# Stores of the last channels asked for on two queues, a broadcast read from 16 rows, and four pairs of loads joined

## The chip, the cores and the metric

The kernel runs on one core of one Trainium2 chip. The metric is the device time of one execution in microseconds. A profiled execution also has a span, from its first to its last instruction, which is a little shorter than its time. The engines are named as in the profile: PE is TensorE (PEld its weight loads), DVE is VectorE, ACT is ScalarE, POOL is GpSimd, SP is the sync engine. An engine name with a q (SPq, ACTq) stands for what the engine's own sequencer does, above all asking for transfers.

## What is computed

Two branches work on the same input of 2048 rows and 512 channels and are mixed by a gate:

```python
x = A_u
g = sigmoid((x * gate_w).sum(-1, keepdims=True))
a = state_space(x)        # kernel K[d, l] = Re sum_n C B dt exp(dt A l); y = irfft(rfft(K, 2L) * rfft(u, 2L))[:L] + u * Dskip
b = linear_attention(x)   # 32 heads of 16; phi = [softmax(p), softmax(-p)]; o = phi_q (phi_k^T v) / (phi_q . sum phi_k + 1e-6); o @ wo
return g * a + (1 - g) * b
```

In a, the convolution kernel has 2048 taps for each channel and comes from 128 complex states. In b, every query row is divided by its own normaliser, one number for each head.

## The kernel before, in words

**An order written out by hand.** The class `Plan` collects nodes: an engine, a function that issues instructions, what it depends on. `Plan.ORDER` is a string that holds the sequence of all nodes, two characters for each. Every engine executes its own nodes in this sequence, and a node that waits holds up what is behind it on its engine. Where a node may run on one of two engines, the next digit of `Plan.SIDES` picks the first (0) or the second (1). Digits are used up in the order in which the nodes were added, not in the order of execution. `Plan.dma` (line 128) adds a transfer as three nodes: the request, which an engine's sequencer issues, and two empty ones for its movement and its landing. In the kernel before, all transfers are requests on SP.

**The input's spectrum** is worked out early and written to the DRAM tensor XUd. Later `load` (line 1178) reads it back in tiles XUX of 128 x 2 x 1024. For the first three quarters of the channels, a tile comes in two requests of 256 KB at line 1186, and for the last quarter in two at line 1188: one request for each of the two halves `i`, which are the same rows shifted by 64.

**The attention queries** (`plan_queries`) run in four blocks of 512 rows. `block` takes exponentials (Eq), forms the sums of all heads in one PSUM tile, and works out on ScalarE and VectorE one factor for each row, head and sign: the normaliser apm, 128 partitions of 256 numbers. A partition stands for (i, h, m): the 128-row group i, head h of eight in a group, and m of four groups. It must be copied to all 16 features of a head. For this apm is written to DRAM (apd, line 895) and read back (ax, line 902): one load for each i, in which each of 8 rows of 1024 numbers is read 16 times. VectorE then multiplies Eq by ax (line 909), two multiplications for each block. Block 3 is the late one, and its stores are at line 991.

**The convolution** (`plan_conv`) runs over the channels in chunks of 32 (units 0 to 15). `kgen` builds the taps (matmuls at line 179) and their spectrum, `transform` multiplies by XUX (line 1289, 1292 or 1227), goes back through psz (line 1315) and stores the result in DRAM (Zd, line 1330), from where ZT is read (line 1349) with other axes on the partitions. The matmuls at line 1378 finish the inverse transform on top of what the attention left, VectorE multiplies by the gate (line 1389) into xT, and the stores at line 1400 write xT to the output. Quarters 0 to 2 hold four units each. The last quarter is split: units 12 and 13 together, then 14, then 15. There are two groups of stores in it, four requests each: after units 12 and 13 for their 64 channels, and after unit 15 for the 64 channels of 14 and 15. One request takes 32 of the 128 partitions and writes 512 pieces of 128 bytes. Line 1400 uses ScalarE's queue when the node's engine is ACT and SP's otherwise; before the change no digit is spent on it and the engine is SP.

**The order around the end.** The last nodes are, in sequence: the stores of the earlier quarters, VectorE's transposes and multiplications by the gate, ScalarE's two last copies of Zr, the four stores of block 3 (line 991), the four of units 12 and 13, VectorE's last three multiplications (line 1389), and the last four stores.

Of the kernel before, what the change touches and what calls it, by code (L numbers as in the profile page):

```python
# [10 lines left out]
ACT = mybir.ActivationFunctionType  # L11
ALU = mybir.AluOpType
F32 = mybir.dt.float32
BF16 = mybir.dt.bfloat16
# [56 lines left out]
class Plan:  # L71
# [738 lines left out]
def plan_queries(P, nc, g, psum, r):  # L810

    fc, act, at, xT = g.fc, g.act, g.at, g.xT
# [12 lines left out]
    def block(b, late, yn=()):  # L825
# [68 lines left out]
        def aw():  # L894
            nc.sync.dma_start(out=g.apd[b].rearrange("i h m c -> (i h m) c"), in_=Q.apm[:].rearrange("p s t -> p (s t)"))
            Q.apm = None

        def ar(ip):
            if ip == 0:
                Q.ax = g.fpool.tile([128, 4, 4, 2, 128], BF16, name="ax", tag="ax", bufs=g.P.k["ax"])  # L900
            for i in (2 * ip, 2 * ip + 1):
                nc.sync.dma_start(out=Q.ax[:, i].rearrange("p m s t -> p (m s t)"),
                                  in_=g.apd[b, i].rearrange("h m c -> h (m c)").unsqueeze(1).to_broadcast([8, 16, 1024]))
        n = P.dma("aw" + L, 0.45, 2.0, aw, [n], drop=["nrm"], move=0.3)
        em, ld = [], None
# [9 lines left out]
        for ip in range(2):  # L915
            for mp in range(1 if late else 2):
# [21 lines left out]
                ot.append(evict("oT" + L, oe, [po, wo]))  # L938

        def out_mm(ps, i, j):  # L940
            for m in range(4):
                nc.tensor.matmul(ps, lhsT=g.oT[3][i // 2][:, m, 128 * (i % 2):128 * (i % 2) + 128], rhs=g.wo[:, m, :], start=(m == 0), stop=False,
                                 skip_group_check=True)
            nc.tensor.matmul(ps[:, 384:512], lhsT=xT[:, j, 3, :], rhs=at.diagD[:, 3, :], start=False, stop=True, skip_group_check=True)
            nc.tensor.matmul(ps[:, 0:384], lhsT=g.ident[:], rhs=g.Y[:, i].rearrange("p q d -> p (q d)"), start=False, stop=True, skip_group_check=True)
        if not late:
            box = Bag()

            def pbm(box=box):
                box.ps = g.heat(g.psA.tile([128, 4, 128], F32, name="bps", tag="bk"), 3)  # L950
                for i in range(4):
                    attn(box.ps[:, i], 4 * b + i, 3, i == 0, True)

            def bs(box=box):
                i = box.ps[:]
                box.ps = None
                return xT[:, 4 * b:4 * b + 4, 3, :], i
            pb = P.add("PE", "bpsq", pbm, ot + [wo], take=["bk"], rw=("diagD", ""))
            out.append(evict("bs3", bs, [pb] + g.xTr))
            g.ot[b] = ot + [wo]  # L960
        on = []
        for ip in range(2 if late else 0):
# [11 lines left out]
            def bg(k, j=j, box=box):  # L974
                o, i = xT[:, j + k, 0:3, :].rearrange("p k d -> p (k d)"), box.ps[:, k, 0:384]
# [12 lines left out]
        if late:  # L988
            def st(h):
                for c in (2 * h, 2 * h + 1):  # L990
                    (nc.scalar if P.cur.at == "ACT" else nc.sync).dma_start(out=g.out2d[:, 0:384].rearrange("(q j c) d -> c q j d", q=32, j=16, c=4)[c][:, 4 * b:4 * b + 4],
                                      in_=xT[32 * c:32 * c + 32, 4 * b:4 * b + 4, 0:3, :].rearrange("p j a d -> p j (a d)"))
# [38 lines left out]
def plan_exp(P, nc, g, psum, U, T, psq, deps):  # L1031
# [5 lines left out]
    def pe():  # L1037
        T.E = g.epool.tile([128, 2, 32, 32], BF16, name="E", bufs=g.P.k["E"])
        box.ps = psum([128, 2, 16, 32], "args")
        for e in range(2):  # L1040
            nc.tensor.matmul(box.ps[:, e], lhsT=g.statE[64 * e:64 * e + 64, h, :], rhs=g.selE[64 * e:64 * e + 64, 16 * cc:16 * cc + 16, :],  # L1041
                             start=True, stop=True, tile_position=(64 * e, 0))

    def ex():
        act(out=T.E[:, 1], in_=box.ps[:].rearrange("p e x t -> p (e x) t"), func=ACT.Exp)
        box.ps = None

    def el():
        nc.vector.tensor_tensor(out=T.E[:, 0].rearrange("p c (t k) -> p c t k", k=2), in0=T.E[:, 1].rearrange("p c (t k) -> p c t k", k=2),
                                in1=g.G[:, 32 * U:32 * U + 32].unsqueeze(2).to_broadcast([128, 32, 16, 2]), op=ALU.mult)  # L1050
# [5 lines left out]
def plan_conv(P, nc, g, psum, r):  # L1056
# [121 lines left out]
    def load(Q, p):  # L1178
        L = Bag()
        L.ring, L.left = "XUX", 2  # L1180

        def dma():
            L.X = g.fpool.tile([128, 2, 1024], BF16, name="XUX", tag="XUX", bufs=g.P.k["XUX"])
            for i in range(2):
                if Q < 3:
                    nc.sync.dma_start(out=L.X[:, i].rearrange("p (h z) -> p h z", h=2), in_=g.XUd[Q, :, 64 * i:64 * i + 128, 8 * p:8 * p + 8, :].rearrange("h x r c -> x h (r c)"))
                else:
                    nc.sync.dma_start(out=L.X[:, i], in_=g.XUd[Q, p // 2, 64 * i:64 * i + 128, 16 * (p % 2):16 * (p % 2) + 16, :].rearrange("x r c -> x (r c)"))
        src = [(h, 8 * p + 4) for h in range(2)] if Q < 3 else [(p // 2, 16 * (p % 2) + r) for r in (4, 12)]
        L.n = P.dma("xup", 0.9, 2.0, dma, [g.XUn[k] for k in src] + [sk], take=["XUX"], move=1.9, cnt=2)  # L1190
        return L

    def transform(XA, ready, Q, off, nd, Ls, last, co=0, free=True, split=False):
# [4 lines left out]
        nh, w = max(1, nd // 64), min(nd, 64)  # L1198
        pair = 1 if Q == 1 else 0
        lo = 64 if last else off  # L1200
# [151 lines left out]
        for j0 in range(0, 16, nj):  # L1352
# [3 lines left out]
            def pya(j0=j0, box=box):  # L1356
                box.ps = psum([128, 2, 512], "psy")
                box.py = box.ps[:].rearrange("p b (r d) -> p b r d", d=nd)
                for i in range(nj):
                    j, o = j0 + i, box.py[:, i // 4, i % 4]  # L1360
                    if j < 12:
# [22 lines left out]
            def ou(j0=j0, box=box):  # L1384
                gb = g.gT[:, j0:j0 + nj]
                if Q < 3 and j0:
                    nc.vector.tensor_tensor(out=bS[:, 8:12, do], in0=box.py[:, 0], in1=g.gT[:, 8:12].unsqueeze(2).to_broadcast([128, 4, nd]), op=ALU.mult)
                    return
# [8 lines left out]

            def st(h, js=slice(0, 12 if Q < 3 else 16)):
                for c in (2 * h, 2 * h + 1):
                    (nc.scalar if P.cur.at == "ACT" else nc.sync).dma_start(out=ov[c][:, js], in_=xT[32 * c:32 * c + 32, js, Q - pair:Q + 1, lo:off + nd].rearrange("p j a d -> p j (a d)"))  # L1400
            ya = []
            if Q < 3:
                ya = [P.add("PE", "pya", pya, [sq] + [n for b in range(j0 // 4, min(3, j0 // 4 + 2)) for n in g.ot[b]] + ([y] if j0 else []), take=[psq], rw=("diagD", ""))]
# [3 lines left out]
            two = Q < 3 and j0 > 0  # L1407
# [4 lines left out]
            if end and Q != 0 and (nd > 32 or last):  # L1412
                for h in range(2):
                    P.dma("out", 1.2, 2.0, lambda h=h, st=st: st(h), on, move=(1.6 if pair else 1.05 if nd == 128 else 0.9), cnt=2)
                on.clear()

    for h in range(6):
# [6 lines left out]
        done = done + kgen((2 * h, 2 * h + 1), XA, h % 2 == 0)  # L1424
        if h % 2:
            transform(XA, done, h // 2, 0, 128, [load(h // 2, p) for p in range(4)], False)
    for n in yn:
        n.deps.append(g.half)
    for u in range(12, 16):
        if u in g.PHASES:  # L1430
            phase(range(u, g.PHASES[u]))
    late += r["block"](3, True, yn)
    L, first = [load(3, p) for p in range(4)], None
# [11 lines left out]
def full_kernel(tc, A_u, A_A_re, A_A_im, A_B_re, A_B_im, A_C_re, A_C_im, A_log_dt, A_Dskip,  # L1445
                B_x, B_wqkv, B_w_phi, B_wo, gate_w, out):
    nc = tc.nc
# [5 lines left out]
    with ExitStack() as ctx:  # L1453
# [192 lines left out]
```

## Time and profile before

| | |
|---|---|
| median of 3 runs | 253.25 us (253.02 to 254.99) |
| time of the profiled execution | 253.31 us |
| its span | 251.4 us |
| TensorE clock granted | 0.961 of full speed |
| bytes moved by the DMA engines | 35.39 MB, mean 141 GB/s |

A timeline line reads: start in us from the start of the span, duration, engine, line of the kernel, operation, output<-input, count, and in brackets the idle time ahead of it and what ended that. For a transfer on SPq the duration is that of the request on the sequencer and not of the movement. A line of a list by tile gives the least, the median and the greatest duration in ns, and the first and the last start. A line of the stretches gives from and to, length, busy time of each engine with its count of instructions, then TensorE's granted clock, the mean busy share of the 16 DMA engines (transfers overlap, so it can pass 1) and GB/s. A line of a list of waits reads: who waited, for whom, us in total, times, the longest.

### The profile page before, as it was taken

How to read it: one execution, taken by the hardware profiler on the slowest of the kernel's cores; microseconds unless marked ns; L12 is line 12 of the kernel's file. 1: busy time of each engine (PE TensorE's matmuls, PEld its weight loads, DVE VectorE, ACT ScalarE, POOL GpSimd, SP SyncE). 2: the span in 40 equal slices, each digit the busy share in tenths (PEclk: the TensorE clock that was granted, in tenths of full speed). 3: DMA queues.
4: the chain of work that ended last, by engine and by line, in shares of the span. 5: the costliest groups of instructions: out<-in, count | busy, mean ns of one | idle time of the engine just before them, and what ended most of it. 6: DMA issues, size and time to landing. Idle time of an engine off the chain costs nothing.

```text
span 251.4 us, 9921 instructions
## 1 busy us (share of the span) xinstructions
PE 203.1 (81%) x4436; PEld 141.4 (56%) x4436; DVE 233.7 (93%) x322; ACT 222.4 (88%) x306; POOL 6.3 (3%) x15
## 2 busy tenths in 40 slices
PE   0567899999966378798878778899998789999970
PEld 0466655456743344255556646775667566777550
DVE  6799999999899997999999999999999999999690
ACT  6699899999989999999999999999999899975330
POOL 5310000000000000000000000000000000000000
PEclk9999999999997759999999999999999999999995
DMA  6799200037290488400325226904786678998775
GB/s 158 158 204 176 83 4 3 21 109 190 55 257 3 125 240 227 169 3 4 117 76 190 85 80 195 289 25 122 175 199 167 201 235 218 215 252 170 179 170 81
DMA packets 62122, 35.39 MB, mean 141 GB/s; under 512 B 41984, under 2 KB 57984, under 8 KB 61696
## 3 DMA queue, kind: packets, MB, share of 16 engines
q1 hardware_dynamic: 62080, 34.76, 54.5%
q8 instruction: 34, 0.56, 0.9%
q14 instruction: 8, 0.07, 0.1%
HBM read 21.91 MB, written 12.85 MB: 138 GB/s over the span
## 4 chain that ended last, share of the span: by engine, by line
ACT 34%; PE 23%; DVE 17%; DMA 10%; SPq 8%; issue 6%; ACTq 0%; DVEq 0%
ACT cs L68 8%; DMA ZT<-Zd 5%; ACT Eq L68 4%; ACT XA L145 4%; ACT E L68 4%; SPq L1512 4%; PE kps L179 3%; PE vp L753 3%; ACT L65 3%; PE pk L705 3%; PE psB L612 2%; DVE Zk L732 2%; ACT Zr L145 2%; SPq L212 2%; DMA UD<-in_A_u_dram 2%
## 5 line engine op out<-in xcount | busy, mean ns | idle before, releaser
L179 PEld LDWEIGHTS <-A 128*32 128x32 bf16 x1664 | 28.5, 160 | 6.6 <-issue 3.8
L179 PE MATMUL kps<-R,A 128*32 128x64 bf16 x1664 | 30.2, 228 | 2.2 <-issue 0.6
L68 ACT ACTIVATE cs<-args 128x1024 bf16<-128x1024 f32 x32 | 30.7, 1045 | 0.4 <-PE args L1019 0.3
L1118 DVE TENSOR_TENSOR R<-E,cs 128x2048 bf16<-128x2048 bf16 x16 | 19.5, 1216 | 0.0
L1097 DVE TENSOR_TENSOR A<-Ctab,Dtab 128x2048 bf16<-128x2048 bf16 x16 | 19.5, 1216 | 0.0
L1102 DVE TENSOR_TENSOR A<-Ctab,Dtab 128x2048 bf16<-128x2048 bf16 x16 | 19.5, 1216 | 0.0
L1114 DVE TENSOR_TENSOR R<-E,cs 128x2048 bf16<-128x2048 bf16 x16 | 19.5, 1216 | 0.0
L145 ACT CAST Zr<-psz 128x1024 bf16<-128x1024 f32 (+1 forms) x17 | 16.5, 974 | 2.5 <-issue 1.2
L145 ACT CAST XA<-psA 128x1024 bf16<-128x1024 f32 (+1 forms) x16 | 15.6, 1006 | 3.2 <-PE psA L186 3.2
L753 PE MATMUL vp<-WW,xT 128*128 128x512 bf16 x64 | 18.3, 416 | 0.0
L145 ACT CAST XK<-psB 128x1024 bf16<-128x1024 f32 (+1 forms) x15 | 15.1, 1010 | 3.4 <-PE psB L192 1.9
L612 PE MATMUL psB<-XAu,TB 64*128 64x128 bf16 x256 | 11.8, 249 | 7.3 <-ACT xst L145 5.1
L1289 DVE TENSOR_TENSOR t<-XUX,XK 128x2048 bf16<-128x2048 bf16 x14 | 17.0, 1217 | 0.6 <-ACT XK L145 0.6
L68 ACT ACTIVATE Ek<-pk 128x512 bf16<-128x512 f32 x32 | 16.8, 602 | 0.4 <-PE pk L705 0.2
L68 ACT ACTIVATE E<-args 128x1024 bf16<-128x1024 f32 x16 | 16.8, 1057 | 0.2 <-PE args L1041 0.2
L68 ACT ACTIVATE Eq<-pq 128x512 bf16<-128x512 f32 (+1 forms) x28 | 16.7, 710 | 0.2 <-PE pq L839 0.2
L1315 PE MATMUL psz<-t,TI 128*128 128x512 bf16 x60 | 15.2, 379 | 1.4 <-ACT cs L68 0.5
L839 PE MATMUL pq<-xT,Wqp 128*128 128x512 bf16 x64 | 15.6, 380 | 0.6 <-ACT Eq L68 0.6
L705 PE MATMUL pk<-WW,xT 128*128 128x512 bf16 x64 | 16.0, 380 | 0.0
L612 PEld LDWEIGHTS <-TB 64*128 64x128 bf16 x256 | 9.5, 110 | 11.2 <-issue 11.1
L732 DVE TENSOR_REDUCE Zk<-Ek 128x64 f32<-128x1024 bf16 x12 | 14.0, 1208 | 0.0
L65 ACT ACT_TABLE_LOAD x10 | 12.8, 1283 | 0.2
(215 smaller groups left out, 491.5 us busy)
## 6 DMA issues: line engine op xcount, KB each, us to landing
XUX<-XUd SPq DMA_DIRECT2D x32, 256.0 KB
XUd<-xst SPq DMA_DIRECT2D x8, 512.0 KB
ax<-apd SPq DMA_DIRECT2D x16, 256.0 KB
Zd<-Zr SPq DMA_DIRECT2D x14, 256.0 KB
ZT<-Zd SPq DMA_DIRECT2D x12, 256.0 KB
UD<-in_A_u_dram SPq DMA_DIRECT2D x16, 128.0 KB
XUd<-xst SPq DMA_DIRECT2D x8, 256.0 KB
wqk<-in_B_wqkv_dram SPq DMA_DIRECT2D x1, 1024.0 KB
```

The lines of the kernel that those rows point to most:

```text
L65: return self.nc.scalar.preload_act_table_set(name)
L68: return self.nc.scalar.activation(**kw)
L145: self.nc.scalar.copy(out=o, in_=i)
L179: nc.tensor.matmul(kps[32 * dj:32 * dj + 32, g4, e, :], lhsT=A[:, ka, :, :, d].rearrange("p a b -> p (a b)"), rhs=R[:, kr, d, :], start=(i ...
L612: nc.tensor.matmul(box.ps[:, c2, sl, :], lhsT=fc.TB[rows, b0:b0 + 2].rearrange("p a b -> p (a b)"), rhs=X.t[rows, k, r0 + sl].rearrange("p ...
L705: nc.tensor.matmul(box.ps[:], lhsT=xT[:, st, kt, :], rhs=g.WW[:, kt, :], start=(kt == 0), stop=(kt == 3))
L732: nc.vector.tensor_reduce(out=K.Z[:, u].rearrange("p g h -> p (g h)"), in_=K.E[:, u].rearrange("p g (h f) -> p (g h) f", f=16), axis=mybir ...
L753: nc.tensor.matmul(box.ps[:], lhsT=xT[:, st, kt, :], rhs=g.WW[:, 4 + kt, :], start=(kt == 0), stop=(kt == 3))
L1097: nc.vector.tensor_tensor(out=c.A[:, 0:2].rearrange("p o a b c -> p (o a) b c"), in0=g.C[U // 8][:, 0:2, :, d0 % 256:d0 % 256 + 32].rearra ...
L1102: nc.vector.tensor_tensor(out=c.A[:, 2:4].rearrange("p o a b c -> p (o a) b c"), in0=g.C[U // 8][:, 1:3, :, d0 % 256:d0 % 256 + 32].rearra ...
L1114: nc.vector.tensor_tensor(out=c.R[:, :, :, 32:64], in0=t.E[:, 1].unsqueeze(1).to_broadcast([128, 2, 32, 32]), in1=t.cs[:], op=ALU.mult)
L1118: nc.vector.tensor_tensor(out=c.R[:, :, :, 0:32], in0=t.E[:, 0].unsqueeze(1).to_broadcast([128, 2, 32, 32]), in1=t.cs[:, ::-1, :, ::-1], o ...
```

## The change

The order is the same, and so is the number of nodes. Five things differ:

- The two groups of stores of the last quarter and the stores of block 3 may be asked for by SP or ACT, and `SIDES` has six more digits for them. A digit stands for a node of two requests.
- apm is written twice, side by side, and each of the four loads of a block reads 16 rows eight times each.
- The two requests of a load for the last quarter become one with an access pattern written out by hand.
- The numbers of requests told to the plan follow this (`cnt`); they are not used when the order is given.
- Two switches are new: BOTHE (16 zeros) and NEAR (empty). With these values all the conditions that test them take the old way, and the split of the output matmuls at line 942 gives the same one matmul.

```diff
     SIDES = ("...
-             "0000000000000001001100000000000011011000")
+             "0000000000000001001100000000000100001101100001")
...
+    BOTHE = ("0000000000000000")
+    NEAR = ()
...
         def aw():
-            nc.sync.dma_start(out=g.apd[b].rearrange("i h m c -> (i h m) c"), in_=Q.apm[:].rearrange("p s t -> p (s t)"))
+            for k in range(2):
+                nc.sync.dma_start(out=g.apd[b, :, :, k].rearrange("i h m c -> (i h) m c"), in_=Q.apm[:].rearrange("p s t -> p (s t)"))
...
                 nc.sync.dma_start(out=Q.ax[:, i].rearrange("p m s t -> p (m s t)"),
-                                  in_=g.apd[b, i].rearrange("h m c -> h (m c)").unsqueeze(1).to_broadcast([8, 16, 1024]))
-        n = P.dma("aw" + L, 0.45, 2.0, aw, [n], drop=["nrm"], move=0.3)
+                                  in_=g.apd[b, i].rearrange("h k m c -> (h k) (m c)").unsqueeze(1).to_broadcast([16, 8, 1024]))
+        n = P.dma("aw" + L, 0.45, 2.0, aw, [n], drop=["nrm"], move=0.3, cnt=2)
...
-                P.dma("outL", 1.2, 2.0, lambda h=h: st(h), on, move=0.8, cnt=2)
+                P.dma("outL", 1.2, 2.0, lambda h=h: st(h), on, move=0.8, cnt=2, eng=("SP", "ACT"))
...
-            for i in range(2):
-                if Q < 3:
-                    nc.sync.dma_start(out=L.X[:, i].rearrange("p (h z) -> p h z", h=2), in_=g.XUd[Q, :, 64 * i:64 * i + 128, 8 * p:8 * p + 8, :].rearrange("h x r c -> x h (r c)"))
-                else:
-                    nc.sync.dma_start(out=L.X[:, i], in_=g.XUd[Q, p // 2, 64 * i:64 * i + 128, 16 * (p % 2):16 * (p % 2) + 16, :].rearrange("x r c -> x (r c)"))
+            for i in range(2 if Q < 3 else 0):
+                nc.sync.dma_start(out=L.X[:, i].rearrange("p (h z) -> p h z", h=2), in_=g.XUd[Q, :, 64 * i:64 * i + 128, 8 * p:8 * p + 8, :].rearrange("h x r c -> x h (r c)"))
+            if Q == 3:
+                v = g.XUd[Q, p // 2, :, 16 * (p % 2):16 * (p % 2) + 16, :].rearrange("x r c -> x (r c)")
+                row = v.ap[0][0]
+                nc.sync.dma_start(out=L.X[:], in_=bass.AP(v.tensor, v.offset, [(row, 128), (64 * row, 2), (1, 1024)]))
...
-                    P.dma("out", 1.2, 2.0, lambda h=h, st=st: st(h), on, move=(1.6 if pair else 1.05 if nd == 128 else 0.9), cnt=2)
+                    P.dma("out", 1.2, 2.0, lambda h=h, st=st: st(h), on, move=(1.6 if pair else 1.05 if nd == 128 else 0.9), cnt=2, eng=("SP", "ACT") if Q == 3 else "SP")
...
-        g.apd = dram.tile([4, 4, 8, 4, 256], BF16, name="apd")
+        g.apd = dram.tile([4, 4, 8, 2, 4, 256], BF16, name="apd")
```

More of the change, by code (lines that the diff above doesn't have):

```diff
@@ L959, in block @@
             out.append(evict("bs3", bs, [pb] + g.xTr))
-            g.ot[b] = ot + [wo]
+        g.ot[b] = ot + [wo]
         on = []
@@ L974, in bg @@
             def bg(k, j=j, box=box):
-                o, i = xT[:, j + k, 0:3, :].rearrange("p k d -> p (k d)"), box.ps[:, k, 0:384]
+                o, i = xT[:, j + k, 0:nn, :].rearrange("p k d -> p (k d)"), box.ps[:, k, 0:128 * nn]
                 if P.cur.at == "ACT":
@@ L1042, in pe @@
                              start=True, stop=True, tile_position=(64 * e, 0))
+    both = P.BOTHE[U] == "1"
     def ex():
         act(out=T.E[:, 1], in_=box.ps[:].rearrange("p e x t -> p (e x) t"), func=ACT.Exp)
+        if both:
+            act(out=T.E[:, 0, :, ::-1], in_=box.ps[:].rearrange("p e x t -> p (e x) t"), func=ACT.Exp, scale=-1.0)
         box.ps = None
     def el():
+        if both:
+            return
         nc.vector.tensor_tensor(out=T.E[:, 0].rearrange("p c (t k) -> p c t k", k=2), in0=T.E[:, 1].rearrange("p c (t k) -> p c t k", k=2),
@@ L1198, in transform @@
         nh, w = max(1, nd // 64), min(nd, 64)
-        pair = 1 if Q == 1 else 0
+        pair = 1 if Q == 1 and Q not in P.NEAR else 0
         lo = 64 if last else off
@@ L1360, in pya @@
                     j, o = j0 + i, box.py[:, i // 4, i % 4]
-                    if j < 12:
+                    if j < 12 or Q in P.NEAR:
                         g.attn(o, j, Q, i % 4 == 0, False)
@@ L1385, in ou @@
                 gb = g.gT[:, j0:j0 + nj]
-                if Q < 3 and j0:
+                if Q < 3 and j0 and Q not in P.NEAR:
                     nc.vector.tensor_tensor(out=bS[:, 8:12, do], in0=box.py[:, 0], in1=g.gT[:, 8:12].unsqueeze(2).to_broadcast([128, 4, nd]), op=ALU.mult)
@@ L1396, in oy, with st @@
                 return g.Y[:, :, Q, :], i
-            def st(h, js=slice(0, 12 if Q < 3 else 16)):
+            def st(h, js=slice(0, 12 if Q < 3 and Q not in P.NEAR else 16)):
                 for c in (2 * h, 2 * h + 1):
@@ L1402, in transform @@
             if Q < 3:
-                ya = [P.add("PE", "pya", pya, [sq] + [n for b in range(j0 // 4, min(3, j0 // 4 + 2)) for n in g.ot[b]] + ([y] if j0 else []), take=[psq], rw=("diagD", ""))]
+                ya = [P.add("PE", "pya", pya, [sq] + [n for b in range(j0 // 4, min(3 + (Q in P.NEAR), j0 // 4 + 2)) for n in g.ot[b]] + ([y] if j0 else []), take=[psq], rw=("diagD", ""))]
             y = P.add("PE", "psy%d" % nd, py, ya + rn[:1 + (j0 + nj - 1) // 8] + [sq] + (late if Q == 3 else []) + ([y] if j0 else []),
@@ L1406, in transform @@
                       drop=([["cs", "ax"][nd > 32]] if end else []), rw=("TJ0 TJ1", ""))
-            two = Q < 3 and j0 > 0
+            two = Q < 3 and j0 > 0 and Q not in P.NEAR
             o = P.add("DVE", "ou", ou, (ya or [y]) + [y, g.gate[0]], drop=([] if two else ["psum"]))
@@ L1411, in transform @@
                 yn.append(P.add(("ACT", "DVE"), "Y", lambda oy=oy: P.copy(*oy()), [ya[0], y, o], drop=["psum"]))
-            if end and Q != 0 and (nd > 32 or last):
+            if end and (Q != 0 or 1 in P.NEAR) and (nd > 32 or last):
                 for h in range(2):
-                    P.dma("out", 1.2, 2.0, lambda h=h, st=st: st(h), on, move=(1.6 if pair else 1.05 if nd == 128 else 0.9), cnt=2)
+                    P.dma("out", 1.2, 2.0, lambda h=h, st=st: st(h), on, move=(1.6 if pair else 1.05 if nd == 128 else 0.9), cnt=2, eng=("SP", "ACT") if Q == 3 else "SP")
                 on.clear()
@@ L1425, in plan_conv @@
         if h % 2:
+            if h // 2 in P.NEAR and not late:
+                for n in yn:
+                    n.deps.append(g.half)
+                late += r["block"](3, True, yn)
             transform(XA, done, h // 2, 0, 128, [load(h // 2, p) for p in range(4)], False)
-    for n in yn:
-        n.deps.append(g.half)
+    if not P.NEAR:
+        for n in yn:
+            n.deps.append(g.half)
     for u in range(12, 16):
@@ L1431, in plan_conv @@
             phase(range(u, g.PHASES[u]))
-    late += r["block"](3, True, yn)
+    if not late:
+        late += r["block"](3, True, yn)
     L, first = [load(3, p) for p in range(4)], None
```

14 lines of the change are left out of this document (8 added, 6 removed).

## The prediction

> **What bounds the kernel now.** I read the page first, its busy shares and the busy tenths of the 40 slices.
>
> ```profile
> PE 203.1 (81%) x4436; PEld 141.4 (56%) x4436; DVE 233.7 (93%) x322; ACT 222.4 (88%) x306; POOL 6.3 (3%) x15
> ...
> PE   0567899999966378798878778899998789999970
> ...
> DVE  6799999999899997999999999999999999999690
> ACT  6699899999989999999999999999999899975330
> ```
>
> Through the middle VectorE (93% of the span) and ScalarE (88%) share the limit, and no transfer shortens that. In the last slices all engines fall silent while the span goes on. One slice is 251.4 / 40 = 6.3 us, so this end is worth a closer look. Next the timeline of the sync engine's queue (SPq) over the end, then its single entries (columns: start, us taken to ask for them, what, how many).
>
> ```profile
> 232.26 0.86 SPq L1400 DMA_DIRECT2D out_dram<-xT  x2
> 233.29 2.67 SPq L1349 DMA_DIRECT2D ZT<-Zd  x4
> 236.01 3.75 SPq L1400 DMA_DIRECT2D out_dram<-xT  x6
> 240.15 3.43 SPq L991 DMA_DIRECT2D out_dram<-xT  x4
> 243.69 5.39 SPq L1400 DMA_DIRECT2D out_dram<-xT  x8
> ...
> 248.45 0.63 SPq L1400 DMA_DIRECT2D out_dram<-xT  x1
> ```
>
> The queue asks for transfers nearly without a gap from 232.26 to 243.69 + 5.39 = 249.08. The last eight stores are the two fours of the fourth quarter of channels: first the 64 channels of units 12 and 13, then the 64 of units 14 and 15. Beside them the timelines of VectorE and ScalarE:
>
> ```profile
> 241.08 1.18 DVE L1389 TENSOR_TENSOR xT<-psy,gT 128x1024 bf16<-128x1024 f32 x1
> ...
> 244.99 0.42 DVE L1389 TENSOR_TENSOR xT<-psy,gT 128x256 bf16<-128x256 f32 x1 [0.39 <-PE psy L1378]
> ...
> 241.15 0.59 ACT L145 CAST Zr<-psz 128x512 bf16<-128x512 f32 x1 [0.55 <-PE psz L1243]
> ```
>
> The first four stores had their data at 241.08 + 1.18 = 242.26, the last four at 244.99 + 0.42 = 245.41. The last data is therefore ready 3.67 us before the queue has finished asking. ScalarE's last work ends at 241.74. So **the end is bound by the issue of stores on one queue**, 5.39 / 8 = 0.67 us for each. That the data engines behind the queue are not the limit here is seen in the stretches (the last two columns are the busy share of the DMA engines and GB/s) and in the list of transfers:
>
> ```profile
> 227.00:228.00 1.00, 1.00 (x41) 0.89 (x42) 1.00 (x2) 1.00 (x2) 0.00 (x0) 1.00 1.17 176
> 236.00:243.60 7.60, 6.24 (x192) 3.82 (x193) 7.57 (x12) 3.38 (x6) 0.00 (x0) 1.00 0.84 189
> 245.50:249.00 3.50, 0.00 (x0) 0.00 (x0) 0.00 (x0) 0.00 (x0) 0.00 (x0) 0.50 0.67 98
> ...
> out_dram<-xT SPq DMA_DIRECT2D x8, 64.0 KB
> ```
>
> 64 KB in 0.67 us is 65,536 / 0.67 = 98 GB/s, just the rate of the last stretch. The engines took more at other times: 176 GB/s with a full share (1.17, transfers overlap) at 227 to 228.
>
> The profiled execution itself took 253.31 us, 1.91 more than its span of 251.40. The median of the three runs is 253.25, so sums against 253.31 hold for it within 0.1.
>
> **The change part by part.** *The last eight stores.* The six new digits in the list of sides read 0 0 for the four stores of the fourth query block (they stay on SP), 0 1 for units 12 and 13, 0 1 for the last four. So of each four two stay and two go to ScalarE's queue. They are the last entries of ScalarE's program; behind the waiting store stands only the other store, and no other engine waits for them. ScalarE is free at 241.74, so its first pair can go at 242.26 and is asked for by about 242.3 + 1.34 = 243.6. SP's pair follows the four L991 stores as now: 243.69 + 2 x 0.67 = 245.03, before the last data at 245.41. Then both queues ask for two each: 245.45 + 2 x 0.67 = 246.79 instead of 249.08, which takes off 2.29 us. What is late next is VectorE's L1389 at 245.41.
>
> The data engines have then 4 x 65,536 = 262,144 bytes to move. At 176 GB/s this is 1.49 us, where two queues offer it in 1.34, so 0.15 comes back. Net: 2.14.
>
> ScalarE's price for asking is not in this trace, since no transfer is asked for there. The nearest row is SP's own:
>
> ```profile
> L1400 SPq DMA_DIRECT2D out_dram<-xT x16: 349/624/984, 232.3 to 248.4; - x16
> L991 SPq DMA_DIRECT2D out_dram<-xT x4: 316/717/1202, 240.2 to 242.4; - x4
> ```
>
> At the least, 0.35 each, it would finish before SP's pair and gain nothing more. At the most, 1.20 each, it finishes at 245.45 + 2.40 = 247.85, which leaves a gain of 1.23. I take the median 0.62 with SP's gap, as it is the same kind of store, and take off 0.2 because the end is now the later of two queues: **gain 1.94**.
>
> The other bound is that the two queues cannot be served at once. Then the last four go one after the other from 245.45: 245.45 + 4 x 0.67 = 248.13, a gain of 0.95.
>
> The Trainium skill speaks for this bound: Perfetto Trace Analysis, "DMA Instruction — HWDGE (DVE, Sync)", says that a sequencer locks one shared generator of descriptors for its own use and that the profile's time of an issue holds that lock. By it the gain is 0.95; with two generators it is the 1.94 above. One queue asks here, so the trace can't decide; the row that leans towards it is that an issue of 512 pieces takes 0.62 and one of 128 pieces (L991) as little as 0.32, so part of the price goes with the pieces.
>
> *The normaliser.* It is now written twice (four more issues in the kernel, one for each block of queries) and read as 16 rows, eight copies each, where it was 8 rows and 16 copies.
>
> ```profile
> L895 SPq DMA_DIRECT2D apd<-apm x4: 332/342/980, 118.7 to 187.4; - x4
> L902 SPq DMA_DIRECT2D ax<-apd x16: 574/586/1211, 120.3 to 194.8; - x16
> L909 DVE TENSOR_TENSOR Eq<-Eq,ax x8: 1211/1216/1219, 126.9 to 203.0; 128x2048 bf16<-128x2048 bf16 x8
> ...
> 123.00:126.00 3.00, 1.75 (x60) 1.08 (x54) 3.00 (x4) 2.98 (x7) 0.00 (x0) 1.00 0.52 170
> 201.00:202.40 1.40, 1.11 (x42) 0.84 (x41) 0.82 (x2) 1.40 (x2) 0.00 (x0) 1.00 1.04 342
> ```
>
> Between 123 and 126 these reads run alone, at a share of 0.52 and 170 GB/s; other loads reach 1.04 and 342. It looks as if eight rows keep half of the engines busy and sixteen would keep all: the 1 MB of a block (four loads of 256 KB) would take 3.1 us for 6.2. A further write costs 0.34 to 0.98 us of queue, and its landing may delay the reads by as much. VectorE does not wait for a transfer anywhere in this execution; its longest waits, and the whole list behind them, name engines only:
>
> ```profile
> DVE xT L147 <- PE xps L500: 2.2, 1, 2.2
> DVE xT L147 <- PE bps L945: 1.2, 1, 1.2
> ...
> PE psy L1378 <- DMA ZT<-Zd: 0.8, 2, 0.6
> ```
>
> So the multiplication L909 stands in VectorE's order and not behind its load: sooner is worth 0. Without that cover the extra write would cost up to 4 x 0.98 = 3.9, against 3.1 saved in each block; as the saving is larger in every block, I count 0 from both sides.
>
> *The joined loads.* Four times one request takes the place of two, same bytes.
>
> ```profile
> L1188 SPq DMA_DIRECT2D XUX<-XUd x8: 399/458/1522, 180.2 to 230.1; - x8
> 228.49 2.00 SPq L1188 DMA_DIRECT2D XUX<-XUd  x2
> ```
>
> Each saves SP about 0.46. The last pair ends at 230.49 and SP then idles until VectorE's result lets it go at 232.26, so 0.46 disappears in 1.77 us of idling. The four fewer requests cancel the four more writes.
>
> The remaining edits (the switches BOTHE and NEAR, all zeros and empty) issue the same instructions as before: 0.
>
> **Sum:** 253.31 - 2.14 + 0.2 = 251.37, and 0.06 lower for the median: **251.3 us**.
>
> **The rivals.** *One generator for both queues:* 253.31 - 0.95 = 252.36, say 252.3. For it: the price goes with the pieces. Against: at 128 pieces half of the 0.62 remains and could overlap. The same time results if only the pair of units 12 and 13 went to ScalarE and the last four stayed on SP, that is, if the digits fell otherwise than I count them.
>
> *The middle gets shorter too:* TensorE waits twice for ZT, 0.8 us in total, in a stretch where it is the limit. The chain that ended last goes through both:
>
> ```profile
> 203.00 1.23 DVE Eq L909
> 204.25 0.32 SPq L1349
> 204.61 6.24 DMA ZT<-Zd
> 210.89 0.63 PE psy L1378 x32
> ```
>
> If less traffic ahead let ZT land sooner, up to 0.8 more goes: 251.37 - 0.8 = 250.57, say 250.5. Against: ZT is asked for when L909 gives its buffer free, which stays at 204.25.
>
> *Nothing at the end:* ScalarE's first requests on a fresh queue cost so much (2.29 / 2 = 1.15 above SP's 0.67 each) that it finishes at 249.08 too: 253.3. No row shows such a price except the single 1.20.
>
> *Slower:* two queues write 128-byte pieces at once and the data engines fall behind. Place: the last four stores, 245.45 on. The store issue now ends 2.32 before the span does, so the change turns into a loss when 262,144 bytes need more than 251.40 - 2.32 - 245.45 = 3.63 us, below 72 GB/s. At half of today's 98 it is 5.35 us and the time 253.31 + 1.72 = 255.0. Against: such pieces went at 176 GB/s at 227 to 228.
>
> **How the numbers follow.** Chances: forecast 0.57, one generator 0.22, shorter middle 0.12, nothing 0.05, slower 0.04. The range 250.3 to 252.6 holds the first three with the bounds of ScalarE's price (1.23 to 2.14) and leaves out some 0.12. About 1% (2.5 us) is what a measurement of this kernel can tell from no change. Faster than 250.7 needs the shorter middle and a little of the forecast's own spread: 0.15. Slower than 255.8 is the tail of the last rival: 0.03. Within 1%: 0.82.
>
> **What would show it.** In the profile after, four L1400 entries stand on ScalarE's queue; the last two on each queue start near 245.45 and run side by side at about 0.65 each, and the span ends near 249.4. If they take turns, or each takes about 1.3, one generator serves both. DMA share in the reads of the normaliser near 1 instead of 0.52 shows the 16 rows, with VectorE's L909 starting at unchanged times. The forecast is wrong if the last L1389 doesn't end near 245.4, because then the middle moved, or if the last request ends near 246.8 and the span much later than 2.4 us after it.

## The result, and the profile after

The changed kernel takes 256.77 us (median of 13 runs, 255.49 to 258.26) where the kernel before takes 254.99 (13 runs, 253.02 to 256.97). The ratio is 1.0082, with a 95% interval of 1.0055 to 1.0109: **0.8% slower**, where the forecast was 0.8% faster. Of the 5.5 us between the forecast of 251.3 and 256.77, 1.7 are the base: the three runs at hand had a median of 253.25, the 13 runs have 254.99. The profiled execution took 255.74 us with a span of 253.9.

The page of the kernel after, the same rows as before: busy time and share, then the tenths of the 40 slices.

```profile
PE 201.9 (80%) x4411; PEld 141.9 (56%) x4436; DVE 234.3 (92%) x322; ACT 222.2 (88%) x306; POOL 6.0 (2%) x15
...
PE   0468799999966578798777978889998689998950
...
DVE  6799999989899998999999999999999899997860
ACT  6799899999999999999999999998998999972600
...
q10 hardware_dynamic: 2112, 0.26, 0.7%
```

VectorE and ScalarE are as busy as before (25 matmul records are missing). A second queue of transfers, q10, is new: 0.26 MB, the four stores on ScalarE. The end is where to look. The timeline of SP's queue over it:

```profile
232.88 0.86 SPq L1413 DMA_DIRECT2D out_dram<-xT  x2
233.97 1.71 SPq L1362 DMA_DIRECT2D ZT<-Zd  x4
235.73 4.55 SPq L1413 DMA_DIRECT2D out_dram<-xT  x6
245.38 1.99 SPq L997 DMA_DIRECT2D out_dram<-xT  x4
248.84 2.67 SPq L1413 DMA_DIRECT2D out_dram<-xT  x4
```

Lines have moved: L991, L1389 and L1400 of before are L997, L1402 and L1413. The same stretch on ScalarE and VectorE:

```profile
240.16 0.59 ACT L983 ACTIVATE xT<-bps,gT 128x384 bf16<-128x384 f32 x1
...
242.91 4.42 ACTq L1413 DMA_DIRECT2D out_dram<-xT  x4
```

```profile
241.70 1.19 DVE L1402 TENSOR_TENSOR xT<-psy,gT 128x1024 bf16<-128x1024 f32 x1
...
245.59 0.42 DVE L1402 TENSOR_TENSOR xT<-psy,gT 128x256 bf16<-128x256 f32 x1 [0.38 <-PE psy L1391]
```

Up to here nearly all is as before. The last data is ready at 245.59 + 0.42 = 246.01, which is 0.6 later than before (245.41). But SP asks for nothing between 235.73 + 4.55 = 240.28 and 245.38, though ScalarE's data for the block 3 stores (L997) was there at 240.16 + 0.59 = 240.75. Before, these stores started at 240.15. The waits of SP's queue from 225 on name the cause:

```profile
SPq L997 <- DMA out_dram<-xT: 5.0, 1, 5.0
...
SPq L1413 <- DMA out_dram<-xT: 1.8, 2, 1.4
```

SP waits 5.0 us **for a store to land** (its own data was there 0.5 us into this wait), and a store reads nothing that another store writes. In the profile before no store waited for another; the one row of that form there is the wait for all transfers at the kernel's end (L1641, 1.2 us). I call the time from the last data to the end of the span the tail. It was 251.4 - 245.41 = 5.99 us and is 253.9 - 246.01 = 7.89; the forecast was 5.99 - 1.94 = 4.05.

The built program tells what is waited for. A request tells of its landing through one of eight semaphores. They are taken in turn by the requests of SP and of ScalarE together, and a request waits until the one that had its semaphore before has landed. The program hands them out at build time, in an order of its own, and there ScalarE's four stores stand ahead of SP's block 3 stores. The last two turns of the kernel after, read from its list of instructions ("second quarter": SP's stores of 32x12x256):

```
semaphore   the turn before                            last turn
0           ACT, 1st store of the last eight           SP, block 3, 1st
1           SP, second quarter                         SP, block 3, 2nd
2           ACT, 2nd store                             SP, block 3, 3rd
3           SP, second quarter                         SP, block 3, 4th
4           ACT, 3rd store                             SP, units 12 and 13, 1st
5           ACT, 4th store                             SP, units 12 and 13, 2nd
6           SP, second quarter                         SP, units 14 and 15, 1st
7           SP, second quarter                         SP, units 14 and 15, 2nd
```

The trace fits it line by line. ScalarE's first store is asked for at 242.91, when its data is there (241.70 + 1.19 = 242.89), and SP's block 3 goes at 245.38, 2.47 later. ScalarE's third store waits for the last data, is asked for at 246.05, and SP's first store of units 12 and 13 goes at 248.84, 2.79 later. The trace records for every request the semaphore that it raises, and the time of each raise. The semaphores 0 to 7 of the table stand there as 100, 101, 102, 105, 106, 108, 109 and 110, in the same turns. ScalarE's first store has landed by them at 245.31 and its third at 248.78, so each of these two requests of SP goes within 0.1 us of the landing that it needs. From issue to landing such a store takes that long; the transfers listed from 240 on, with KB and the median us to landing (block 3 first, then ScalarE's stores):

```profile
out_dram<-xT SPq DMA_DIRECT2D x4, 96.0 KB, 2.2
out_dram<-xT ACTq DMA_DIRECT2D x4, 64.0 KB, 2.6
```

In the kernel before, the previous holder of every semaphore was a request of SP itself, a whole turn older, and by the same records it had landed 2 us or more before its semaphore was needed.

The Trainium skill, DMA: Bandwidth & Descriptors, "Why a DMA increments its semaphore by 16 and not by 1", gives a reason for such waits: with two transfers in flight on one semaphore its count doesn't say which of them is complete. No run here shows what would go wrong without the wait; the trace shows its price.

### The profile page after: what moved, and what is told of

It reads as the page before. It is cut to its first block, busy times and chain, and to the rows that moved or that the text cites. A ratio compares the mean times of both kernels' runs of the same rounds, so it can differ in the third digit from the quotient of the medians.

```text
span 253.9 us, 9905 instructions
## 1 busy us (share of the span) xinstructions
PE 201.9 (80%) x4411; PEld 141.9 (56%) x4436; DVE 234.3 (92%) x322; ACT 222.2 (88%) x306; POOL 6.0 (2%) x15
## 4 chain that ended last, share of the span: by engine, by line
DVE 32%; ACT 26%; PE 18%; issue 8%; SPq 7%; DMA 5%; DVEq 0%; ACTq 0%
ACT cs L68 5%; ACT Eq L68 4%; DVE t L1302 4%; SPq L1531 3%; PE psB L614 3%; DVE R L1126 3%; DVE A L1109 3%; PE pk L707 3%; PE vp L755 3%; ACT E L68 3%; DVE Zk L734 2%; SPq L214 2%; DVE R L1130 2%; ACT XA L147 2%; ACT L65 2%
## 5 line engine op out<-in xcount | busy, mean ns | idle before, releaser
L614 PE MATMUL psB<-XAu,TB 64*128 64x128 bf16 x256 | 12.8, 261 | 6.4 <-ACT xst L147 4.2
L755 PE MATMUL vp<-WW,xT 128*128 128x512 bf16 x59 | 17.1, 406 | 0.8 <-issue 0.7
L1328 PE MATMUL psz<-t,TI 128*128 128x512 bf16 x49 | 14.6, 380 | 2.1 <-ACT cs L68 0.5
L614 PEld LDWEIGHTS <-TB 64*128 64x128 bf16 x256 | 10.3, 116 | 10.4 <-issue 10.2
```

Source lines behind the costliest of these rows:

```text
L614: nc.tensor.matmul(box.ps[:, c2, sl, :], lhsT=fc.TB[rows, b0:b0 + 2].rearrange("p a b -> p (a b)"), rhs=X.t[rows, k, r0 + sl].rearrange("p ...
L755: nc.tensor.matmul(box.ps[:], lhsT=xT[:, st, kt, :], rhs=g.WW[:, 4 + kt, :], start=(kt == 0), stop=(kt == 3))
```

## The experiments

My theory is that of **the turns**: the loss is SP's requests waiting for stores that ScalarE asks for late. The first rival is that of the record, **two queues** that write 128-byte pieces at once are slow by themselves. The second is that the other two edits make **the middle** slower. Executions differ by some us in the middle, before any store of the end is reached (the last data is ready between 244.9 and 249.1). So beside the ratio I read the tail of each profile, from the last multiplication by the gate to the end of the span. There is one profile for each kernel; with all eight stores on SP the tails are 6.0, 6.4 and 5.6, so a difference below some 0.8 says little.

| kernel | last eight stores | ratio, 95% interval | last data, us | tail, us |
|---|---|---|---|---|
| before | 8 SP | 1 | 245.41 | 6.0 |
| after | 4 SP, 4 ACT | 1.0082 [1.0055, 1.0109] | 246.01 | 7.9 |
| e1_all_sp | 8 SP | 0.9999 [0.9961, 1.0038] | 245.80 | 6.4 |
| e2_queue_alone | 4 SP, 4 ACT | 1.0071 [1.0034, 1.0107] | 244.90 | 8.0 |
| e3_last_pair | 6 SP, 2 ACT | 1.0107 [1.0053, 1.0161] | 246.24 | 8.8 |
| e4_pool | 4 SP, 4 POOL | 0.9961 [0.9926, 0.9996] | 248.43 | 5.0 |
| e5_q1_early | 4 SP, 4 ACT, other order | 1.0006 [0.9970, 1.0041] | 246.64 | 5.5 |
| e6_q1_early_all_sp | 8 SP, other order | 1.0004 [0.9964, 1.0043] | 248.56 | 5.6 |
| e7_early_six | 2 SP, 6 ACT, other order | 0.9961 [0.9919, 1.0002] | 249.09 | 4.2 |
| e8_early_eight | 8 ACT, other order | 0.9998 [0.9966, 1.0029] | 247.14 | 5.1 |
| e9_eight | 8 ACT | 1.0041 [1.0001, 1.0080] | 246.55 | 6.1 |

In the diffs below a minus is the kernel after, unless said otherwise.

**e1_all_sp: all stores back on SP.** The new normaliser and the joined loads stay.

```diff
-             "0000000000000001001100000000000100001101100001")
+             "0000000000000001001100000000000000001101100000")
```

> All stores asked for by SP again; the normaliser as 16 rows and the joined loads stay. Three theories. Turn theory: the loss is that both queues take the same eight completion semaphores in turn, so that SP's four stores of block 3 wait for the landing of ScalarE's first store; with one queue no such wait is left: ratio 0.997 to 1.003, L997 starts about 0.6 us after the last scaling on ScalarE begins, and from the end of the last L1402 to the end of the span it is 6.0 us as before (7.9 in the changed kernel). Two-queue theory (a second queue slows the issue or the writes themselves): the same here. Middle theory (the 16 rows or the joined loads delay the middle by the 0.6 us by which the last L1402 ends later, and the end by more): 1.002 to 1.008, with the last L1402 later than before by 0.5 us or more.

Measured: 0.9999. The timeline at the end, SP and then VectorE:

```profile
240.55 3.84 SPq L997 DMA_DIRECT2D out_dram<-xT  x4
244.49 5.36 SPq L1413 DMA_DIRECT2D out_dram<-xT  x8
```

```profile
245.38 0.42 DVE L1402 TENSOR_TENSOR xT<-psy,gT 128x256 bf16<-128x256 f32 x1 [0.39 <-PE psy L1391]
```

Block 3 starts at 240.55 again, and the loss is gone. The other two edits are worth nothing that can be measured.

**e2_queue_alone: only the change of the queue,** on the old normaliser and the old loads (a minus is the kernel after).

```diff
-            for k in range(2):
-                nc.sync.dma_start(out=g.apd[b, :, :, k].rearrange("i h m c -> (i h) m c"), in_=Q.apm[:].rearrange("p s t -> p (s t)"))
+            nc.sync.dma_start(out=g.apd[b].rearrange("i h m c -> (i h m) c"), in_=Q.apm[:].rearrange("p s t -> p (s t)"))
...
-                                  in_=g.apd[b, i].rearrange("h k m c -> (h k) (m c)").unsqueeze(1).to_broadcast([16, 8, 1024]))
+                                  in_=g.apd[b, i].rearrange("h m c -> h (m c)").unsqueeze(1).to_broadcast([8, 16, 1024]))
...
-            for i in range(2 if Q < 3 else 0):
+            for i in range(2):
...
```

> Only the queues are changed; normaliser with 8 rows and loads in two, as before. Turn theory: ratio 1.006 to 1.011, SP's first L996 waits for a landing of out_dram until about 2.4 us after ScalarE's first store was asked for, and 7.9 us from the last multiplication by the gate to the end. Two-queue theory: the same ratio. Middle theory: 0.990 to 0.995, since the expected gain at the end would show.

Measured: 1.0071, and the same picture:

```profile
244.26 2.00 SPq L996 DMA_DIRECT2D out_dram<-xT  x4
247.78 2.70 SPq L1411 DMA_DIRECT2D out_dram<-xT  x4
```

```profile
241.79 4.43 ACTq L1411 DMA_DIRECT2D out_dram<-xT  x4
```

```profile
SPq L996 <- DMA out_dram<-xT: 4.9, 1, 4.9
```

ScalarE's first store goes at 241.79, SP's block 3 at 244.26, again 2.47 behind it. The theory of the middle is out: the queue alone brings the whole loss.

**e3_last_pair: only the very last two stores on ScalarE's queue.**

```diff
-             "0000000000000001001100000000000100001101100001")
+             "0000000000000001001100000000000000001101100001")
```

> Only the very last two stores stay on ScalarE's queue, those of units 12 and 13 go back to SP. In the program SP's first store of units 12 and 13 then waits for the semaphore that ScalarE's first last store takes. Turn theory: the loss grows although fewer stores are moved: that store can start only at the landing, about 2.4 us after ScalarE's request at 0.05 after the last L1402, and six stores of 0.67 follow: 2.4 + 4.0 + 2.3 = 8.7 us from the end of the last L1402 to the end of the span, ratio 1.009 to 1.013. Two-queue theory: half as much on the second queue, half the loss or less: 1.000 to 1.005. Middle theory: below 1.002.

Measured: 1.0107.

```profile
246.27 1.37 ACTq L1413 DMA_DIRECT2D out_dram<-xT  x2
```

```profile
240.99 3.47 SPq L997 DMA_DIRECT2D out_dram<-xT  x4
248.57 4.02 SPq L1413 DMA_DIRECT2D out_dram<-xT  x6
```

```profile
SPq L1413 <- DMA out_dram<-xT: 4.0, 1, 4.0
```

Half as many stores are moved, and the loss doesn't shrink. The stores of block 3 are free now (240.99), but ScalarE's first store, which can't be asked for before the last data, holds the semaphore that SP's first store of units 12 and 13 needs. That one goes at 248.57, 2.30 behind ScalarE's, and takes five more with it. SP asks for nothing while ScalarE asks for its two, so the two-queue rival has hardly a place for a loss here.

**e4_pool: the same four stores, asked for by GpSimd,** which has semaphores of its own (111 to 114 in the trace's records).

```diff
...
-                    (nc.scalar if P.cur.at == "ACT" else nc.sync).dma_start(out=ov[c][:, js], in_=xT[32 * c:32 * c + 32, js, Q - pair:Q + 1, lo:off + nd].rearrange("p j a d -> p j (a d)"))
+                    (nc.gpsimd if P.cur.at == "POOL" else nc.sync).dma_start(out=ov[c][:, js], in_=xT[32 * c:32 * c + 32, js, Q - pair:Q + 1, lo:off + nd].rearrange("p j a d -> p j (a d)"))
...
-                    P.dma("out", 1.2, 2.0, lambda h=h, st=st: st(h), on, move=(1.6 if pair else 1.05 if nd == 128 else 0.9), cnt=2, eng=("SP", "ACT") if Q == 3 else "SP")
+                    P.dma("out", 1.2, 2.0, lambda h=h, st=st: st(h), on, move=(1.6 if pair else 1.05 if nd == 128 else 0.9), cnt=2, eng=("SP", "POOL") if Q == 3 else "SP")
```

> The same two pairs of stores as in the changed kernel are asked for by GpSimd, whose transfers take semaphores of their own (SP's are then only its own again). Turn theory: SP's L997 are not held up and start where they did before; SP ends its two last stores 1.4 us after the last L1402; what GpSimd takes to ask is not known, with 0.7 each the span ends 4 us after the last L1402 and the ratio is 0.990 to 0.995, with 2 us each it is 1.000. Two-queue theory (writes of two queues side by side are slow): L997 start early but the span still ends 7 us or more after the last L1402, ratio 1.004 or more.

Measured: 0.9961, **faster than both kernels**, though a little less than expected. SP, GpSimd, and VectorE's last multiplication:

```profile
243.20 2.61 SPq L997 DMA_DIRECT2D out_dram<-xT  x4
245.91 3.81 SPq L1413 DMA_DIRECT2D out_dram<-xT  x4
```

```profile
246.01 1.49 POOL L1413 DMA_DIRECT2D out_dram<-xT  x2 [233.09 <-DVE xT L1402]
248.73 1.26 POOL L1413 DMA_DIRECT2D out_dram<-xT  x2 [1.23 <-DVE xT L1402]
```

```profile
248.01 0.42 DVE L1402 TENSOR_TENSOR xT<-psy,gT 128x256 bf16<-128x256 f32 x1 [0.36 <-PE psy L1391]
```

SP waits for no store. Same stores, same pieces, two queues, and no loss: what cost time was not the second queue. The tail is 253.4 - 248.43 = 5.0.

**e5_q1_early: the changed kernel with other turns.** The four stores of the second quarter are moved forward in ORDER, and the turns fall otherwise. ScalarE's stores hold semaphores 4, 6, 1, 3; block 3 gets 5, 7, 0, 2; SP's last four get 4, 5, 6, 7.

```diff
-              "...dydzdAfbfc"
-              "fdg0fjfk...fRgderfsbRbSbTgcesbU"
-              "bVbWgffSfT...")
+              "...dydzdAbRbS"
+              "bTbUbVbWfbfcfdg0fjfk...fRgderfs"
+              "gcesgffSfT...")
```

> The changed kernel with all its sides kept (two of each of the last fours on ScalarE's queue), but the four stores of the second query quarter's 32x12x256 tiles are asked for some 14 us sooner in the written order, so that the turns of the eight completion semaphores fall otherwise: ScalarE's four stores share none with the four 32x4x384 stores ahead on SP's queue. Theory of the turns: SP's 32x4x384 stores start near 241 again and not near 245.4; its stores of units 12 and 13 share their semaphores with ScalarE's first two and start near 245.4, its last two near 246.7; the end is about 2 us sooner than with all stores on SP, ratio 0.990 to 0.995. Theory that two queues of 128-byte pieces are slow by themselves: the same stores go to the same two queues, so it stays slower, 1.005 to 1.010.

Measured: 1.0006, a miss for both theories. SP, then ScalarE's requests:

```profile
241.28 3.04 SPq L997 DMA_DIRECT2D out_dram<-xT  x4
246.50 2.67 SPq L1413 DMA_DIRECT2D out_dram<-xT  x4
```

```profile
243.53 4.56 ACTq L1413 DMA_DIRECT2D out_dram<-xT  x4
```

The mechanism did as foretold: block 3 is free at 241.28, and SP's units 12 and 13 wait for ScalarE's first store alone. The size did not. That wait ended 2.97 behind ScalarE's request and not 2.47, and the span ended 252.1 - 249.17 = 2.9 behind the last request and not 2.4. SP's four requests ended 249.17 - 246.64 = 2.5 behind the last data, where two take 1.3. What was left of the wait, with the slower landing, used the gain up.

**e6_q1_early_all_sp: the control, the same order with all on SP.**

```diff
-             "0000000000000001001100000000000100001101100001")
+             "0000000000000001001100000000000000001101100000")
```

> The control of the run before: the same order with the four earlier stores, and all stores on SP's queue. Both theories: 0.998 to 1.002, since the end is again eight requests of about 0.67 us behind one another on SP. If it is faster by itself, what the run before gains belongs to the order and not to the second queue.

Measured: 1.0004, as expected. The order by itself makes no difference that can be measured. (The profiled execution took 256.85 us, more than the median of 255.31; its last data is late, at 248.56, and its tail is 5.6.)

**e7_early_six: the same order, all of units 12 and 13 and half of the last four on ScalarE.** SP's last two then follow ScalarE's first two in the turns, which have landed by the time the data comes.

```diff
-             "0000000000000001001100000000000100001101100001")
+             "0000000000000001001100000000001100001101100001")
```

> The same order, and six of the last eight stores on ScalarE's queue: all four of units 12 and 13 and two of the last four; SP keeps the other two. SP's last two share their semaphores with ScalarE's first two, which land by about 246, when the last data comes anyway. Theory of the turns: no wait for another queue's store of more than about 0.3 us; the last four requests go side by side from about 246 and end by 247.4, the span some 2.4 us behind: 2.4 to 2.8 us less than with all on SP, ratio 0.988 to 0.992. Theory that two queues of 128-byte pieces are slow by themselves: slower, 1.005 or more.

Measured: 0.9961, faster by a third to a half of what was expected, with the upper end of the interval just above 1, so it is not quite clear of no change. VectorE's last multiplication, then ScalarE's and SP's last requests from 249 on:

```profile
248.67 0.42 DVE L1402 TENSOR_TENSOR xT<-psy,gT 128x256 bf16<-128x256 f32 x1 [0.50 <-PE psy L1391]
```

```profile
249.13 1.26 ACTq L1413 DMA_DIRECT2D out_dram<-xT  x2
```

```profile
249.13 1.56 SPq L1413 DMA_DIRECT2D out_dram<-xT  x2
```

This is the picture that the prediction drew: both queues start 0.04 behind the last data (249.09), two requests each, side by side. The tail is 4.2, where the forecast had 4.05. The two-queue rival wanted 1.005 or more and is out. Against its control the tail is 1.4 us shorter (0.5%), and the ratios differ by 0.4%, though their intervals overlap; I had expected 2.4 to 2.8 us, reckoned from e1's tail of 6.4 instead of this order's 5.6.

**e8_early_eight and e9_eight: all eight on ScalarE,** once in the other order and once in the order of the changed kernel. One queue writes the 128-byte pieces, and only the turns differ.

```diff
-             "0000000000000001001100000000000100001101100001")
+             "0000000000000001001100000000001100001101100011")
```

> The order with the four earlier stores, and all of the last eight stores on ScalarE's queue, none on SP: one queue alone writes 128-byte pieces, as in the kernel before. Theory of the turns: no store waits for one that is asked for late on the other queue; ScalarE starts when the data of units 12 and 13 is there and not behind SP's 32x4x384 stores. Eight requests of about 0.68 us from that data, some 2.35 us from the last request to the end of the span, and 3.2 us between the first and the last data give a tail behind the last data of 5.45 + 2.35 - 3.2 = 4.6 us, where it is 5.6 to 6.4 with all on SP: 1.0 to 1.8 us less, ratio 0.993 to 0.998. Theory that two queues of 128-byte pieces are what costs: the same as with all on SP, 0.998 to 1.002.

> The same eight stores on the same queue as in the run before, none of them on SP, but in the order of the changed kernel. Only the turns of the semaphores differ: SP's four 32x4x384 stores come behind ScalarE's third and fourth store in the turns, and ScalarE's fifth behind the last of those four. Theory of the turns: SP's first 32x4x384 store starts about 3.8 us behind the data of units 12 and 13, the last some 5.4 behind it, ScalarE's fifth store waits until about 7.8 behind it; with four requests more and 2.35 us the tail behind the last data is about 9.6 us, 3.2 more than with all on SP in this order: ratio 1.008 to 1.015. Theory that two queues of 128-byte pieces are what costs: only one queue writes such pieces, so no loss, 0.998 to 1.002.

Measured: 0.9998 for e8 and 1.0041 for e9. SP's and ScalarE's requests in e8:

```profile
241.90 2.71 SPq L997 DMA_DIRECT2D out_dram<-xT  x4
```

```profile
244.03 5.76 ACTq L1413 DMA_DIRECT2D out_dram<-xT  x8
```

And the same in e9, with SP's longest wait:

```profile
247.24 2.10 SPq L997 DMA_DIRECT2D out_dram<-xT  x4
```

```profile
243.34 5.91 ACTq L1413 DMA_DIRECT2D out_dram<-xT  x8
```

```profile
SPq L997 <- DMA out_dram<-xT: 6.2, 2, 5.9
```

In e9 block 3 is held back until 247.24, 3.9 us behind the data of units 12 and 13 (expected 3.8); in e8 it is not held back. The tails differ by 1.0 us (0.4%) and so do the ratios, though their intervals overlap. ScalarE's last four requests are held back in neither: they end 249.25 - 246.55 = 2.7 behind the last data in e9 and 249.79 - 247.14 = 2.65 in e8. What comes later in e9 is the landing. SP asks for block 3 beside them until 249.34, and the span ends some 3.2 behind that, against 2.4 behind the last request in e8. Both sizes were off. For e8 I had let the eight requests run without a stop, but the fifth needs the last data, so the tail can't be shorter than four requests and the landing. For e9 I had the last step the wrong way round: ScalarE's fifth store comes ahead of block 3's last in the turns and does not wait. With that its tail (6.1) is no longer than e1's (6.4), so its 0.4% over the kernel before isn't explained by the tail; the interval barely leaves out 1, and the cause stays open.

## Why the prediction was wrong

**The step that failed** is this one: "SP's pair follows the four L991 stores as now: 243.69 + 2 x 0.67 = 245.03", together with "no other engine waits for them". In their place stand 245.38 for the four stores of block 3 and 248.84 for SP's pair. I had followed each queue through its own data and its own sequence, and had looked for a dependence between the two only in what they share of hardware. They share the completion semaphores. The two ends account for the whole: the tail is 7.9 instead of 4.05, and the last data 0.6 later, together 4.4, which is 255.74 - 251.37.

**The end is bound by the issue of stores.** Right, and it stayed so: e1 repeats it with 8 requests in 5.36 us, and e7 takes it away.

**Four stores on ScalarE bring 1.94.** Right in mechanism where no turn stands in the way: in e7, with six on ScalarE, the tail is 4.2, 1.8 less than before and 1.4 less than its control. In the other kernels part of it or all went into waits.

**The price of a request on ScalarE, taken from SP's median 0.62.** Right: eight in e8 took 5.76 with a wait for data among them, two in e7 took 1.26. The rival *nothing at the end* needed 0.67 + 1.15 = 1.82 for a request, so the single 1.20 was no row for it, and ScalarE's four in the kernel after took 0.58 to 0.82.

**One generator for both queues** (1.0 lower gain). Wrong. In the kernel after these two pairs run within the same 1.3 us, ScalarE's first and SP's second:

```profile
246.05 1.29 ACTq L1413 DMA_DIRECT2D out_dram<-xT  x2
```

```profile
246.21 1.16 SPq L997 DMA_DIRECT2D out_dram<-xT  x2
```

SP's two took 0.45 and 0.67, within the 0.32 to 1.20 of L991 before. In e7, with 512 pieces on both sides, the four requests are done within 1.56 us, where one queue takes 5.36 / 2 = 2.7 for four (e1); one of SP's took 0.86, so a small price is not excluded. The Trainium skill, Perfetto Trace Analysis, "DMA Instruction — HWDGE (DVE, Sync)", describes a generator shared by two sequencers, under a lock; its heading names VectorE's and SP's, and a note there carries the mechanism over to SP and ScalarE. For ScalarE and SP the trace shows no lock that lasts a whole issue, and the measurement decides.

**The normaliser in 16 rows is worth 0.** Right, and so is the mechanism. One stretch of its reads after, and the same before:

```profile
195.00:198.00 3.00, 2.15 (x68) 1.42 (x68) 3.00 (x4) 2.02 (x3) 0.00 (x0) 1.00 1.01 269
```

```profile
195.00:198.00 3.00, 2.84 (x93) 2.07 (x94) 3.00 (x5) 2.34 (x3) 0.00 (x0) 1.00 0.53 195
```

The share (the last column but one) goes from 0.53 to 1.01, as if all engines worked instead of half. The Trainium skill, DMA: Bandwidth & Descriptors, has the rule for it under "Why a DMA increments its semaphore by 16 and not by 1" (how many engines): the number of engines is the largest up to 16 that divides the slowest axis of both sides, so 8 for 8 rows and 16 for 16; the trace agrees. VectorE's multiplication still starts when its own order lets it, at 126.9 first and 203.8 last (before 126.9 and 203.0), except for one wait of 0.3 us for its load, where there was none before:

```profile
L912 DVE TENSOR_TENSOR Eq<-Eq,ax x8: 1215/1220/1226, 126.9 to 203.8; 128x2048 bf16<-128x2048 bf16 x8
```

**The joined loads are worth 0.** Right: e1 keeps both edits and measures 0.9999.

**Slower, but not by the slower rival.** That one put the loss at "the last four stores, 245.45 on", with data engines that fall behind. The stretches after show engines with time to spare:

```profile
245.38:248.84 3.46, 0.17 (x12) 0.00 (x0) 0.42 (x1) 0.00 (x0) 0.00 (x0) 0.50 0.83 159
248.84:251.51 2.67, 0.00 (x0) 0.00 (x0) 0.00 (x0) 0.00 (x0) 0.00 (x0) 0.50 0.39 56
```

While SP asks for its last four, the share is 0.39 at 56 GB/s; with both queues active just before it was 0.83 at 159. The sides of the table were not to blame: four entries stand on ScalarE's queue, as counted.

The list of what would prove the forecast wrong did not hold the case either. It spoke of the last data and of a span that ends long after the last request; here the last request itself came late.

## What to carry to other kernels

Before a transfer is moved to another queue, read in the built program which completion semaphore it gets, who has that semaphore next, and on which queue: if requests of two queues take turns on one set, an early request can be tied to one that is asked for late. A wait of one store for another store, which share no data, is the sign of it in the list of waits. Move the transfers that become ready first, so that the next holder comes after their landing anyway (e7, whose tail is shorter while its ratio is not quite clear of 1), or use an engine with semaphores of its own (e4).

## What the runs showed of the hardware that was not expected

Requests of SP and ScalarE, 512 pieces each, were issued side by side in 1.26 and 1.56 us for two (e7), where four on one queue take 2.7. Landing was slower when two queues wrote at the end: the span ended 2.6 us behind the last request in e7, 2.9 in e5 and some 3.2 in e9, and 2.4 in the kernels with one queue at the end. Behind GpSimd's last request (248.73 + 1.26 = 249.99 in e4) it took 3.4 us to the end of the span, 1.0 more than the 2.4, and by as much e4's tail of 5.0 is over the expected 4.
